# Seven products for eight in the second FFN product of two of three block pairs

## The chip, the cores and the metric

The kernel runs on one core of one Trainium2 chip. What counts is the device time of one execution in microseconds. TensorE multiplies matrices, VectorE and ScalarE do elementwise work, and SyncE (SP) issues the transfers between the chip's memory (HBM) and the core's own (SBUF). TensorE adds up its results in PSUM banks of 512 float32 columns.

## The reference

The inputs are q, k, v of shape (8, 8, 576, 64), a norm weight, and four matrices U (576, 32), V (32, 576), w_ch1 (512, 2048), w_ch2 (2048, 512).

```python
kv  = einsum('bhsd,bhde->bhse' of q with einsum('bhsd,bhse->bhde', k, v))   # linear attention
x   = kv / sqrt(mean(kv*kv, -1) + 1e-6) * g_norm                           # heads joined: (8, 576, 512)
u   = x + (x^T @ U @ V)^T                                                   # mixes the 576 tokens at rank 32
out = u + relu(u @ w_ch1) @ w_ch2                                           # the FFN
```

The matrices come as 64-bit floats and are cut to 32 bits in the kernel; the result is float32.

## The kernel before

The 8 x 576 tokens are one row of 4608, cut into nine blocks of 512. All work is transposed: features on the 128 partitions, tokens in the free dimension. A product keeps nearly float32 accuracy by splitting both factors into a high and a low part of the type float32r, and adding three matmuls: high x high, high x low, low x high. "Split" below means: ScalarE copies the high part (a cast), VectorE subtracts it from the value to give the low part.

Blocks 0 to 2 run the FFN in the ordinary way. Meanwhile the attention of the next sequences is done in small steps, a `pair_tasks` for each two heads; `at(h, ...)` puts such a step at step number h of the FFN, and `do(h)` emits what stands there. Blocks 3 to 8 run as three pairs, (3, 4), (5, 6) and (7, 8).

In a pair the first product, u @ w_ch1, goes by the Strassen-Winograd scheme. The hidden 2048 features are 16 chunks of 128; chunk n and chunk n + 8 form a *chunk pair*, and the four blocks A11 to A22 of a 2 x 2 matrix are the two chunks by the two halves of the 512 input features. With the other factor's four blocks (two halves of the features by two token blocks) seven products give what eight would: the weight forms `A11 A12 S2 S1 S3 S4 A22` with the forms of u `B11 B21 T2 T1 T3 B22 T4`. Each is 2 x 3 = 6 matmuls for a chunk pair. The weight's sums S1 to S4 are made once, in blocks 1 and 2, by `forms_of_w`, split, and stored in HBM; the forms of u are made by `forms_of_u` before the pair starts and stay in SBUF.

The chunk pairs are taken two at a time (`NPP = 2`), in `NG = 4` groups. For a group, the loop over the seven forms does `product` for both chunk pairs; `after` copies or adds the results into `sums` and, for each of the four hidden blocks 11, 12, 21, 22, runs `relu_to`: high part by ScalarE, low part by VectorE, into `hs`. Two PSUM banks serve a chunk pair, x and y: A11, S2, S3 and A22 add to x; A12 starts y; S1 starts y anew, so it may start only when A12's result has been read; S4 adds to it.

Then the second product of the group, `y_units`: eight units (two token blocks by four output chunks of 128), each 4 x 3 = 12 matmuls with the plain w_ch2, added by VectorE into the pair's running sum r (which starts as u). In the last group the sums go to `st` and out to HBM.

Weight forms come through `ring`, eight slots of 256 KB: `load_form(k + 7)` asks for the piece seven ahead after piece k is used. The w_ch2 chunks of a group (four of 512 KB) come into `w2r` by `load_w2` at the end of the group before. All transfers are on SP's one queue, in order. On each engine the order is set at build time by a scheduler that works from its own costs and from the order of the code; at run time each engine keeps that order. In the tables here `mm` is line 85, `add` line 542, the parts of `relu_to` lines 464 and 465, `load_form` line 520, `load_w2` line 527, and the forms of the weight lines 233 to 244.

Of the kernel before, what the change touches and what calls it, by code (L numbers as in the profile page):

```python
# [10 lines left out]
F32 = mybir.dt.float32  # L11
F32R = mybir.dt.float32r
# [23 lines left out]
STEPS = dict(kv=0, out=2, turn=3, t=5, mix=8)  # L36
STEPS0 = dict(kv=1, out=2, turn=2, t=6, mix=11)
PAIRS = {1: (0, 3, 6, 9), 2: (33, 39, 45, 51), 3: (64, 67, 70, 73), 4: (75, 78, 81, 84),
         5: (98, 103, 109, 114), 6: (120, 125, 131, 136), 7: (162, 169, 176, 183)}
# [4 lines left out]
RING = 8  # L44
FORMS = ["A11", "A12", "S2", "S1", "S3", "S4", "A22"]
# [11 lines left out]
def build(ctx: ExitStack, tc: tile.TileContext, kv_in, kvt0_in, kvt_in, q_in, uv_in, g_in, w_in, out):  # L57
# [7 lines left out]
    st = ctx.enter_context(tc.tile_pool(name="st", bufs=3))  # L65
    dec = ctx.enter_context(tc.tile_pool(name="dec", bufs=2))
# [109 lines left out]
    w1d, w2d = {}, {}  # L176
# [41 lines left out]
    def forms_of_w(n):  # L218

        c = DM // 2  # L220
        a = dec.tile([P, 2 * DM], F32, name="dec")
        for k, f in enumerate((n, n + HALF)):
            if f == 0:
                d1, d2 = [to_dram(f"{which}d0", whole[which, 0]) for which in ("w1", "w2")]
                w = whole["w1", 0]
            else:
                d = to_dram(f"wd{f}", whole[f])
                d1, d2 = d[:, 0:2], d[:, 2:4]
                w = whole[f][:, 0:2]
            w2d[f] = d2  # L230
            for i in range(2):
                w1d[n, f"A{k + 1}{i + 1}"] = d1[:, i]
            nc.vector.tensor_tensor(out=halves(a[:, k * DM:(k + 1) * DM]), in0=w[:, :, 0].bitcast(F32), in1=w[:, :, 1].bitcast(F32), op=ALU.add)
        a11, a12, a21, a22 = (a[:, k * c:(k + 1) * c] for k in range(4))
        ts = {}

        def form(name, in0, in1, op):
            t = ts[name] = st.tile([P, 2, c], F32R, name="st")
            nc.vector.tensor_tensor(out=t[:, 1].bitcast(F32), in0=in0, in1=in1, op=op)
            nc.scalar.copy(out=t[:, 0], in_=t[:, 1].bitcast(F32))  # L240

        def low(name):
            t = ts.pop(name)
            nc.vector.tensor_tensor(out=t[:, 1], in0=t[:, 1].bitcast(F32), in1=t[:, 0].bitcast(F32), op=ALU.subtract)
            w1d[n, name] = to_dram(f"w{name}_{n}", t)

        form("S1", a21, a22, ALU.add)
        form("S2", ts["S1"][:, 1].bitcast(F32), a11, ALU.subtract)
        low("S1")
        form("S4", a12, ts["S2"][:, 1].bitcast(F32), ALU.subtract)  # L250
        low("S2")
        form("S3", a11, a21, ALU.subtract)
        low("S4")
        low("S3")

    ut = {}
    rs = {}

# [603 lines left out]
```

## Time and profile before

| | us |
|---|---|
| median of 3 runs (903.16 to 905.18) | 903.65 |
| profiled execution | 902.88 |
| its span, first to last instruction | 901.1 |
| TensorE busy | 876.8 (97%) |
| VectorE busy | 561.3 (62%) |
| ScalarE busy | 313.5 (35%) |
| share of the transfer engines, main queue | 55.8% |
| mean granted TensorE clock | 0.994 |

Matmuls are pipelined: a row's mean duration (389 ns) is longer than the distance from one to the next, so the price of a matmul is read from a stretch without gaps, its length by its count. The first pair starts near 367 us, the second near 559, the last near 735; the last matmul ends near 898. "PE" is TensorE, "PEld" its weight loads, "DVE" VectorE, "ACT" ScalarE, "SPq" the transfer queue of SP. L85 stands for the line of the kernel, and `y<-hs,w2r` for a matmul from hs and w2r into the bank y.

### The profile page before, as it was taken

The numbers are of one execution on the slowest core, as the hardware profiler recorded it, in microseconds if no ns is written. First come the engines' busy times: TensorE is split into PE (matmuls) and PEld (weight loads), VectorE is DVE, ScalarE is ACT, GpSimd is POOL, SyncE is SP. The second block draws the span as 40 slices with busy tenths as digits, with TensorE's granted clock in tenths as the row PEclk, the third lists the DMA queues.
The fourth block names the chain that finished last, engine by engine and source line by source line (L and its number), as shares of the span: only waits on it lengthen the run. The fifth ranks groups of instructions, "written<-read, shape, count | busy, mean of one in ns | idle before, by whom it ended". The sixth has DMA issues, their size and how long they took to land.

```text
span 901.1 us, 12196 instructions
## 1 busy us (share of the span) xinstructions
PE 876.8 (97%) x4370; PEld 734.7 (82%) x4370; DVE 561.3 (62%) x1089; ACT 313.5 (35%) x629; POOL 22.3 (2%) x43
## 2 busy tenths in 40 slices
PE   8799999989999999999999999999999999999998
PEld 7678878778888878888888888888888888888887
DVE  6999996667866676475647666557452754243342
ACT  5545542333333434433424153324141422213030
POOL 2000002000020000200000000000000000000000
PEclk9899999999999999999999999999999999999999
DMA  9962123998575544766648384748282654527142
GB/s 339 407 263 80 46 79 106 367 381 337 199 232 151 145 118 113 228 188 209 212 147 290 86 267 143 249 124 265 56 254 73 208 194 133 183 75 219 38 164 94
DMA packets 81852, 168.11 MB, mean 187 GB/s; under 512 B 9216, under 2 KB 27392, under 8 KB 79872
## 3 DMA queue, kind: packets, MB, share of 16 engines
q1 hardware_dynamic: 81792, 167.33, 55.8%
q8 instruction: 35, 0.57, 0.3%
q14 instruction: 25, 0.20, 0.1%
HBM read 124.44 MB, written 42.86 MB: 186 GB/s over the span
## 4 chain that ended last, share of the span: by engine, by line
PE 85%; DVE 10%; DMA 2%; issue 1%; SPq 1%; ACT 1%; DVEq 0%; ACTq 0%
PE y L85 64%; PE h L85 11%; PE pp L85 9%; DVE dec L105 1%; DMA ut<-xt 1%; DVE dec L107 1%; DMA kvq<-kv_in 1%; DVE hl L465 1%; DVE ws L113 1%; DVE dec L102 1%; DVE x L338 1%; DVE dec L103 1%; DVE xt L366 0%; DVE ss L326 0%; DVE ut L446 0%
## 5 line engine op out<-in xcount | busy, mean ns | idle before, releaser
L85 PE MATMUL y<-hs,w2r 128*128 128x512 f32 (+1 forms) x1164 | 268.5, 389 | 0.0
L85 PEld LDWEIGHTS y<-hs,w2r 128*128 128x128 f32 x1164 | 215.4, 188 | 43.5
L85 PE MATMUL h<-uth,ws 128*128 128x512 f32 x360 | 122.1, 400 | 3.3 <-DVE hl L465 2.9
L85 PE MATMUL y<-hh,ws 128*128 128x512 f32 x360 | 118.9, 394 | 0.0
L85 PEld LDWEIGHTS h<-uth,ws 128*128 128x128 f32 x360 | 68.3, 190 | 20.2 <-DVE hl L465 6.4
L85 PEld LDWEIGHTS y<-hh,ws 128*128 128x128 f32 x360 | 67.2, 188 | 13.7
L85 PE MATMUL h<-utl,ws 128*128 128x512 f32 x180 | 70.8, 394 | 0.0
L85 PE MATMUL y<-hl,ws 128*128 128x512 f32 x180 | 70.1, 390 | 0.0
L85 PE MATMUL y<-uT,ringw 128*128 128x512 f32 x282 | 67.0, 389 | 0.0
L85 PE MATMUL y<-uT,ring 128*128 128x512 f32 x276 | 65.9, 390 | 0.0
L85 PEld LDWEIGHTS y<-uT,ringw 128*128 128x128 f32 x282 | 52.6, 188 | 10.7
L542 DVE TENSOR_TENSOR uth<-y,uth 128x512 f32<-128x512 f32 x36 | 24.9, 691 | 58.2 <-PE y L85 58.1
L85 PEld LDWEIGHTS y<-uT,ring 128*128 128x128 f32 x276 | 51.5, 188 | 10.6
L542 DVE TENSOR_TENSOR utl<-y,utl 128x512 f32<-128x512 f32 x36 | 24.9, 691 | 48.4 <-PE y L85 48.3
L85 PE MATMUL y<-uB,ring 128*128 128x512 f32 x216 | 52.1, 391 | 0.0
L549 ACT COPY sums<-y 128x512 f32<-128x512 f32 x23 | 13.4, 586 | 108.7 <-PE y L85 108.4
L85 PE MATMUL y<-uB,ringw 128*128 128x512 f32 x210 | 50.4, 391 | 0.0
L542 DVE TENSOR_TENSOR sums<-y,sums 128x512 f32<-128x512 f32 x48 | 32.7, 688 | 23.6 <-PE y L85 18.7
L85 PEld LDWEIGHTS y<-uB,ring 128*128 128x128 f32 x216 | 40.2, 188 | 8.2
L464 ACT ACTIVATE hh<-h 128x512 fp32r<-128x512 f32 x47 | 28.0, 596 | 52.2 <-PE h L85 52.0
L85 PEld LDWEIGHTS y<-uB,ringw 128*128 128x128 f32 x210 | 39.2, 188 | 8.1
L542 DVE TENSOR_TENSOR dec<-y,dec 128x512 f32<-128x512 f32 x23 | 15.9, 692 | 44.8 <-PE y L85 37.9
(200 smaller groups left out, 1208.2 us busy)
## 6 DMA issues: line engine op xcount, KB each, us to landing
w2r<-wd SPq DMA_DIRECT2D x45, 512.0 KB, 6.1
raw<-w_in SPq DMA_DIRECT2D x30, 512.0 KB, 10.2
wd<-ws SPq DMA_DIRECT2D x15, 1024.0 KB, 8.0
kv_sb<-kv_in SPq DMA_DIRECT2D x29, 512.0 KB, 3.9
ring<-wS SPq DMA_DIRECT2D x48, 256.0 KB, 4.5
ringw<-wS SPq DMA_DIRECT2D x48, 256.0 KB, 4.4
ring<-wd SPq DMA_DIRECT2D x36, 256.0 KB, 3.8
out<-st SPq DMA_DIRECT2D x35, 256.0 KB, 2.0
```

The costliest lines, as they stand in the source:

```text
L85: ins = nc.tensor.matmul(*args, **kw)
L102: nc.vector.tensor_scalar(out=tmp, in0=tmp, scalar1=ABS_LO, scalar2=ABS_HI, op0=ALU.max, op1=ALU.min)
L103: nc.vector.tensor_scalar(out=bits, in0=bits, scalar1=3, scalar2=0x3fffffff, op0=ALU.logical_shift_left, op1=ALU.bitwise_and)
L105: nc.vector.scalar_tensor_tensor(out=bits, in0=high, scalar=0xC0000000, in1=bits, op0=ALU.bitwise_and, op1=ALU.bitwise_or)
L107: nc.vector.scalar_tensor_tensor(out=bits, in0=low, scalar=29, in1=bits, op0=ALU.logical_shift_right, op1=ALU.bitwise_or)
L113: lo_eng.tensor_tensor(out=lo, in0=src, in1=hi.bitcast(F32), op=ALU.subtract)
L338: nc.vector.tensor_tensor(out=xv[:, 0:4], in0=s["big"].rearrange("p (i h e) -> p i h e", h=2, e=D), in1=rv[:, 0:4].unsqueeze(3).broadcast_ ...
L464: nc.scalar.activation(out=hh, in_=h, func=AF.Relu)
L465: nc.vector.scalar_tensor_tensor(out=hl, in0=h, scalar=0.0, in1=hh.bitcast(F32), op0=ALU.max, op1=ALU.subtract)
L542: nc.vector.tensor_tensor(out=out, in0=in0, in1=in1, op=ALU.add)
L549: nc.scalar.copy(out=s[0], in_=x)
```

## The change

The second product of pairs (5, 6) and (7, 8) goes by the same seven-product scheme. There the 2 x 2 matrix of the weight has two halves of the 512 outputs by two chunks, and the other factor is the hidden activation with its blocks 11, 12, 21, 22. The pair (3, 4) keeps its form.

- Groups are four chunk pairs (`NR = 4`), two groups a pair. A group does two rounds of the first product, `round_of_ffn1`, two chunk pairs each, and then the seven forms of the second, `product2`: for each form two output chunks i, and for each i the four chunk pairs by three matmuls, 24 matmuls a form, all adding up in one bank for each i.
- `after_both` takes the place of `after`: it leaves the relu'd blocks h11, h12, h22, h21 whole in float32. `form_of_h` then makes the forms of h: "sums1" and "sums2" the differences, three and one VectorE instructions of 1024 columns for two chunk pairs, and for each of the seven forms and each two chunk pairs a split into `entry` tiles (four of them, so a form has two and the next form the other two; two of the four lie in the pools `dec` and `hhl`). The first two forms are split within and just after the rounds, form n + 2 after the product of form n.
- `after2` adds each result to the running sum: 14 adds a group in place of 16 for the same chunk pairs; the last is not cut in two halves any more.
- The weight's sums for the second product are made in the first pair: `sums_of_w("w2", ...)` for each of the eight chunk pairs, from the `w2r` tiles loaded there, in two steps placed between the first pair's units. Step one adds high and low parts back to whole values and makes four differences; step two splits them (`dec`, `wf`) and stores them with two transfers of 512 KB. The sums for the first product are made by the same function now, at every third step in place of every second.
- All weight forms of the last two pairs, for both products, come through the ring in 256 KB pieces: `load_upto(k + 8)`. `w2r` is loaded for the first pair alone.
- Steps of the attention for blocks 5 to 7 move by one, and for blocks 5 to 7 the steps t and mix come two later (`STEPS2`).

```diff
+BOTH = (5, 7)
+NR = 4
...
+        def one():
+            t["plain"] = a = dec.tile([P, 2 * DM], F32, name="dec")
+            for k, w in enumerate(get()):
+                nc.vector.tensor_tensor(out=halves(a[:, k * DM:(k + 1) * DM]), in0=w[:, :, 0].bitcast(F32), in1=w[:, :, 1].bitcast(F32), op=ALU.add)
+            a11, a12, a21, a22 = (a[:, k * c:(k + 1) * c] for k in ((0, 1, 2, 3) if which == "w1" else (0, 2, 1, 3)))
+            for o, in0, in1, op in ((a22, a21, a22, ALU.add), (a21, a11, a21, ALU.subtract), (a11, a22, a11, ALU.subtract),
+                                    (a12, a12, a11, ALU.subtract)):
+                nc.vector.tensor_tensor(out=o, in0=in0, in1=in1, op=op)
+
+        def two():
+            hi = dec.tile([P, 2 * DM], F32R, name="dec")
+            lo = wf.tile([P, 2 * DM], F32R, name="wf")
+            split(hi, lo, t["plain"], nc.vector)
+            d = dram.tile([P, 4, 2, c], F32, name=f"{which}s{n}")
+            for s, part in enumerate((hi, lo)):
+                nc.sync.dma_start(out=d[:, :, s], in_=part.bitcast(F32).rearrange("p (a c) -> p a c", a=4))
...
+    def load_upto(end):
+
+        for k in range(len(loaded), min(end, len(pieces))):
+            t = loaded[k] = sb["ring"][k % RING]
+            nc.sync.dma_start(out=t.bitcast(F32), in_=wd[pieces[k]])
...
+    def form_of_h(name, q):
+
+        two = slice(2 * q, 2 * q + 2)
...
+        if name == "sums1":
+            nc.vector.tensor_tensor(out=h11, in0=h12, in1=h11, op=ALU.subtract)
+            nc.vector.scalar_tensor_tensor(out=t2, in0=h22, scalar=0.0, in1=h11, op0=ALU.max, op1=ALU.subtract)
+            nc.vector.scalar_tensor_tensor(out=h12, in0=h22, scalar=0.0, in1=h12, op0=ALU.max, op1=ALU.subtract)
+        elif name == "sums2":
+            nc.vector.tensor_tensor(out=h21, in0=h21, in1=t2, op=ALU.subtract)
+        else:
+            hi, lo = entries[name, q] = sb["entry"][(2 * WITH.index(name) + q) % len(sb["entry"])]
+            src = {"B11": h11, "B21": h21, "T2": t2, "T1": h11, "T3": h12, "B22": h22, "T4": h21}[name]
...
+                nc.scalar.copy(out=hi, in_=src)
+                nc.vector.tensor_tensor(out=lo, in0=src, in1=hi.bitcast(F32), op=ALU.subtract)
+
+    def product2(k, n, i, bank, first):
+
+        for r in range(NR):
+            w = loaded[k + r].rearrange("p s (i f) -> p s i f", i=2)
+            hi, lo = (t[:, r % 2] for t in entries[WITH[n], r // 2])
+            for m, (s, t) in enumerate(((0, hi), (0, lo), (1, hi))):
+                mm(bank, lhsT=w[:, s, i], rhs=t, start=(first and r == 0 and m == 0), stop=(r == NR - 1 and m == 2),
+                   skip_group_check=not first)
...
+            round_of_ffn1(j, g, 0, after_both)
+            for name in ("B11", "B21"):
+                form_of_h(name, 0)
+            round_of_ffn1(j, g, 1, after_both)
+            form_of_h("B11", 1)
+            form_of_h("B21", 1)
+            form_of_h("sums1", 1)
+            form_of_h("sums2", 1)
...
+                    product2(k, n, i, banks[i, which], FORMS[n] in ("A11", "A12", "S1"))
+                    after2(n, i, banks[i, 0], banks.get((i, 1)), j, g == HALF // NR - 1)
+                k += NR
+                load_upto(k + RING)
+                if n + 2 < len(FORMS):
+                    for q in range(2):
+                        form_of_h(WITH[n + 2], q)
```

Three places show how the change moves instructions. The first is TensorE at the end of the last pair. Before, the last form of the first product (uT with a ring slot) is followed by units that take hs and w2r; the last rows of the kernel are these:

```order
L85 MATMUL y<-hs_3574,w2r_3577 128x512 x3
L85 MATMUL y<-hs_3572,w2r_3576 128x256 x3
L85 MATMUL y<-hs_3572,w2r_3577 128x256 x3
L85 MATMUL y<-hs_3574,w2r_3576 128x256 x3
L85 MATMUL y<-hs_3574,w2r_3577 128x256 x3
```

Now, from the last form of the last round on:

```order
L90 MATMUL y<-uT_3007,ringw_2535 128x512 x12
L90 MATMUL y<-entry_5177,ring 128x512 x6
L90 MATMUL y<-entry_5178,ring 128x512 x6
L90 MATMUL y<-entry_5177,ring 128x512 x6
L90 MATMUL y<-entry_5178,ring 128x512 x6
L90 MATMUL y<-dec,ringw_2534 128x512 x6
L90 MATMUL y<-hhl,ringw_2535 128x512 x6
```

Each form takes 24 matmuls from two of the four entry tiles, and the ring's slots now feed both products.

The second place is VectorE in the first pair, where one group's units end and the next group's first forms are read. L542 into uth is the unit's add, L542 into sums the add that reads A12's bank (line 556 after the change); ss, ta, r and x are steps of the attention. Before:

```order
L542 TENSOR_TENSOR uth<-y,uth 128x512
L326 TENSOR_REDUCE ss<-x 128x10
L542 TENSOR_TENSOR sums<-y,sums 128x512
L328 RECIPROCAL r_4481<-ta 128x10
L329 TENSOR_TENSOR ta<-r_4481 128x10
L330 SCALAR_TENSOR_TENSOR ta<-ss,ta 128x10
L542 TENSOR_TENSOR sums<-y,sums 128x512
```

Now, from right behind the last unit's add:

```order
L248 TENSOR_TENSOR dec<-w2r_3427 128x512
L397 TENSOR_TENSOR t_4357<-pp,t_4357 32x128
L336 TENSOR_REDUCE ss<-x 128x10
L248 TENSOR_TENSOR dec<-w2r_3427 128x512
L338 RECIPROCAL r_4371<-ta 128x10
L252 TENSOR_TENSOR dec<-dec 128x256
L339 TENSOR_TENSOR ta<-r_4371 128x10
L252 TENSOR_TENSOR dec<-dec 128x256
L340 SCALAR_TENSOR_TENSOR ta<-ss,ta 128x10
L252 TENSOR_TENSOR dec<-dec 128x256
L341 SCALAR_TENSOR_TENSOR r_4371<-ta,r_4371 128x10
L556 TENSOR_TENSOR sums<-y,sums 128x512
```

Two adds that read the new group's w2r (L248) and three of the differences (L252) have come between the last unit's add and the add that reads A12's bank.

The third is VectorE behind the second product of the last pair, from the first results on:

```order
L556 TENSOR_TENSOR uth<-y,uth 128x512
L639 TENSOR_TENSOR h_5175<-h_5175,t_5176 128x1024
L648 TENSOR_TENSOR entry_5177<-t_5176,entry_5177 128x1024
L556 TENSOR_TENSOR uth<-y,uth 128x512
L648 TENSOR_TENSOR entry_5178<-t_5176,entry_5178 128x1024
L556 TENSOR_TENSOR st<-y,uth 128x512
L648 TENSOR_TENSOR dec<-h_5172,dec 128x1024
```

Low parts of 1024 columns (L648) alternate with the adds of results, where before only the units' adds stood.

More of the change, by code (lines that the diff above doesn't have):

```diff
@@ L228, in forms_of_w @@
                 d1, d2 = d[:, 0:2], d[:, 2:4]
-                w = whole[f][:, 0:2]
+                ws.append(whole[f][:, 0:2])
             w2d[f] = d2
             for i in range(2):
[L232 to L240, printed above, removed]
@@ L458, in relu @@
     def relu(h):
[L459 to L461 removed]
+        t = hp.tile([P, 2, BLK], F32R, name="hhl")
+        relu_to(t[:, 0], t[:, 1], h)
+        return t[:, 0], t[:, 1]
     def relu_to(hh, hl, h):
@@ new lines, in product2, with after2 @@
+    def product2(k, n, i, bank, first):
[5 more added lines that the diff above has]
+                   skip_group_check=not first)
+    def after2(n, i, x, y, j, last):
+        name = FORMS[n]
+        src = y if name in ("A12", "S1", "S4") else x
+        part = int(name in ("S2", "S1", "S3", "S4"))
+        c = i + 2 * int(name in ("S1", "S3", "A22"))
+        own = r_of(j + part)[:, c]
+        if last and name in ("A12", "S3", "S4", "A22"):
+            o = st.tile([P, DM], F32, name="st")
+            add(o, src, own)
+            nc.sync.dma_start(out=out[j + part, c], in_=o)
+        else:
+            add(own, src, own)
@@ L774, in build, with round_of_ffn1 @@
     h = 32 * NSTD
-    for j in range(NSTD, NBLK, 2):
-        for g in range(NG):
+    def round_of_ffn1(j, g, q, done):
+        nonlocal k, h
+        banks = {}
+        for n in range(len(FORMS)):
+            do(h)
+            h += 1
+            for a in range(2):
+                early = k == 0
+                if n == 0:
+                    banks[a, 0] = ps_p.tile([P, BLK], F32, name="pp") if early else ps_y.tile([P, BLK], F32, name="y")
+                elif n == 1:
+                    banks[a, 1] = ps_y.tile([P, BLK], F32, name="y")
+                which = int(FORMS[n] in ("A12", "S1", "S4"))
+                product(k, n, banks[a, which], FORMS[n] in ("A11", "A12", "S1"))
+                k += 1
+                if early:
+                    ffn2(y_prev, [hprev])
+                    finish(y_prev, NSTD - 1)
+                    sb_tiles("rest")
+                    sb_tiles("ring2")
+                    load_w2(0)
+                done(n, 2 * q + a, banks[a, 0], banks.get((a, 1)))
+                load_upto(k + RING)
+            if q == 1 and n in (1, 3):
+                form_of_h(f"sums{n // 2 + 1}", 0)
```

157 lines of the change are left out of this document (93 added, 64 removed).

## The prediction

> **What bounds the kernel now.** I read the page's first part, then the windows over the last three pairs of blocks, then the chain of waits and TensorE's own waits.
>
> ```profile
> PE 876.8 (97%) x4370; PEld 734.7 (82%) x4370; DVE 561.3 (62%) x1089; ACT 313.5 (35%) x629; POOL 22.3 (2%) x43
> PEclk9899999999999999999999999999999999999999
> ```
>
> ```profile
> core 0: us, PE busy (x) PEld busy (x) DVE busy (x) ACT busy (x) POOL busy (x), PEclk, DMA share, GB/s
> 150.00:200.00 50.00, 47.43 (x249) 39.85 (x247) 32.54 (x75) 15.98 (x39) 4.68 (x4) 1.00 0.93 354
> ...
> 405.00:570.00 165.00, 164.38 (x830) 138.32 (x829) 102.03 (x205) 60.39 (x122) 0.00 (x0) 1.00 0.63 200
> 570.00:736.00 166.00, 166.00 (x799) 138.87 (x798) 94.33 (x172) 51.38 (x98) 0.00 (x0) 1.00 0.51 161
> 736.00:901.00 165.00, 162.09 (x727) 134.52 (x725) 59.42 (x89) 34.02 (x56) 0.00 (x0) 1.00 0.42 141
> ```
>
> The last three rows are most of the first pair, the second (from near 559 us) and the third. TensorE is busy through all of them, at full clock, while VectorE falls from 62% to 57% to 36%. The chain of waits ends in one unbroken stretch of TensorE, and its waits from 405 us to the last matmul come to 0.6 us:
>
> ```profile
> 666.74 231.36 PE y L85 x1032
> ```
>
> ```profile
> PE pp L85 <- DVE xh L354: 0.6, 1, 0.6
> ```
>
> So in the pairs the time is the number of matmuls times their spacing. Of the 1032, 24 have half the columns, so 231.36 / 1020 = 0.2268 us for each full one. What the change removes there is worth its full spacing, as long as the new forms, sums and loads keep up.
>
> **The change, part by part.**
>
> *1. Fewer matmuls.* One pair's second product takes 4 groups x 8 units x 12 = 384 full matmuls now, and 2 groups x 7 forms x 2 x 12 = 336 after. Two pairs: 96 fewer, 96 x 0.2268 = **-21.8 us**. The first product keeps its 336. Lower bound: if the spacing were not the matmul's own but that of what feeds it, a removed one would be worth the weight load's 188 ns, 96 x 0.188 = 18.0 us.
>
> ```profile
> L85 PEld LDWEIGHTS y<-hs,w2r 128*128 128x128 f32 x1164 | 215.4, 188 | 43.5
> L465 DVE SCALAR_TENSOR_TENSOR hs<-sums,hs 128x512 fp32r<-128x512 f32 x48 | 32.7, 687 | 2.5 <-ACT hs L464 1.3
> ```
>
> The Trainium skill (TensorE: Matmul & The Clock Gate, section Back-to-back issue gap) has a sustained spacing of about 131 ns for 512 columns in a stream of weight loads and matmuls; by it the saving would be 96 x 0.131 = 12.6 us, an estimate from that page. This trace does not agree (0.2268 us over 1020 matmuls), and the measurement decides.
>
> *2. Work for VectorE and ScalarE in the last two pairs.* Prices:
>
> ```profile
> L113 DVE TENSOR_TENSOR ws<-dec,ws 128x1024 fp32r<-128x1024 f32 x15 | 18.2, 1219 | 0.7 <-ACT ws L112 0.6
> L542 DVE TENSOR_TENSOR uth<-y,uth 128x512 f32<-128x512 f32 x36 | 24.9, 691 | 58.2 <-PE y L85 58.1
> L244 DVE TENSOR_TENSOR st<-st 128x256 fp32r<-128x256 f32 x32 | 13.1, 422 | 3.8 <-ACT st L240 2.9
> ```
>
> ```profile
> L112 ACT CAST ws<-dec 128x1024 fp32r<-128x1024 f32 x15 | 15.8, 1051 | 24.5 <-DVE dec L107 17.5 <-DVE ta L330 4.8 <-DVE r L331 2.1
> L464 ACT ACTIVATE hs<-sums 128x512 fp32r<-128x512 f32 x48 | 30.2, 631 | 25.9 <-DVE sums L542 25.8
> ```
>
> Per pair VectorE loses 32 low parts of 512 (32 x 0.687 = 22.0) and 4 adds (2.8), and gains 28 low parts of 1024 (28 x 1.219 = 34.1) and 16 sums of 1024 (19.5): +28.8 us. The last pair goes from 59 to 88 us busy of about 154 (57%), the second from 94 to 123 of about 155 (79%). ScalarE gains 28 casts of 1.051 and loses 8 relus of 0.631, +24 us: 75 of 155 at most. Neither becomes the bound on average; what counts is whether a form is late at its place.
>
> In the second product each form is 24 matmuls, 24 x 0.2268 = 5.44 us. Behind it VectorE must do two low parts and two adds, 2 x 1.219 + 2 x 0.691 = 3.8 us, and ScalarE two casts, 2.1 us; a form's first tile is free at three quarters of the product two before, so cast, low part, cast, low part have 1.4 + 5.4 us for 1.05 + 2 x 1.22 plus waits. In the last pair that leaves over 2 us. In the second pair the attention of block 7 runs on VectorE too. Adding rows in program order I find the narrowest places in its second group: S1 of the second round restarts a bank whose reading add ends 0.4 us earlier, and T3's second half is ready 1.5 us before its use. Bounds: 0 (all fit) to 6 us (two late forms in each of the two groups, each by one 1.219 us and wait); I take **+1**, nearer the row sums, which fit.
>
> *3. The second-product forms, made in the first pair.* For each of 8 chunk pairs VectorE gets two adds of 512, four of 256 and one low part of 1024: 2 x 0.691 + 4 x 0.422 + 1.219 = 4.3 us, in all 34 us, and ScalarE one cast. VectorE's 102 us of 165 becomes about 131 (80%). SP gets 16 stores of 512 KB. The cost is in the order: the two adds that read w2r's new contents stand ahead of the adds of A12, and VectorE works in order. So a late weight load now holds VectorE, then A12's bank, then S1, which starts that bank anew. Before, the loads had until the end of the seven forms. The group from 467 us:
>
> ```profile
> 467.19 2.06 SPq L527 DMA_DIRECT2D w2r<-wd  x4
> 468.74 2.88 PE L85 MATMUL y<-uB,ring 128*128 128x512 f32 x12
> 474.16 0.69 DVE L542 TENSOR_TENSOR sums<-y,sums 128x512 f32<-128x512 f32 x1
> 475.54 0.69 DVE L542 TENSOR_TENSOR sums<-y,sums 128x512 f32<-128x512 f32 x1 [0.16 <-PE y L85]
> 475.61 5.61 PE L85 MATMUL y<-uT,ringw 128*128 128x512 f32 x24
> ```
>
> ```profile
> L527 SPq DMA_DIRECT2D w2r<-wd x12: 319/351/444, 416.0 to 518.9; - x12
> DMA to landing us min/median/max: 3.9/6.5/9.0
> ```
>
> The third of the four loads is issued at about 468.2 and lands at 474.7 (median) or 477.2 (longest). Then come the second w2r add, three differences and the small statistics (0.69 + 1.27 + 0.5 = 2.5), A12's first add (0.69, ends 477.9 or 480.4) and, after 0.42 + 0.96, the second (479.9 or 482.4). S1 starts at about 475.61 + 2.72 = 478.35, its second half at 479.7. So TensorE waits 0.2 us at the median and 2.7 us at the longest. Three such places: 0 to 8 us. I take 1 each, **+3**, between the median and the longest because the stores load the queue further. The first group's loads are issued long before its start, and VectorE's wait for an output transfer there gives cover.
>
> *4. Loads in the last two pairs.* A pair loads 112 pieces of 256 KB, 29.4 MB, in 672 x 0.2268 = 152 us: 193 GB/s, beside 354 that the 150 to 200 us row shows at a share of 0.93. A piece of the second product frees its slot in the second half of its form, and the piece that takes the slot is wanted 33 matmuls or 7.5 us later. Landing times now:
>
> ```profile
> L520 SPq DMA_DIRECT2D ring<-wd x36: 319/320/422, 379.2 to 865.3; - x36
> ...
> DMA to landing us min/median/max: 2.7/4.4/8.2
> ```
>
> The median leaves 3 us, which hides it, with SP's issue at about 0.4 us each. A longest one costs 0.7. Bounds 0 to 2; I take 0. Without that cover every form would wait (a rival below).
>
> *5. The first-product forms* in blocks 1 and 2 are spread over every third step, with one low part of 1.219 for four of 0.422 and one cast for four. VectorE saves 0.5 us a chunk pair. TensorE's idle time from 100 to 400 us, most of those blocks, is 300 less 291.99:
>
> ```profile
> 100.00:200.00 100.00, 96.45 (x481) 79.07 (x479) 75.53 (x147) 36.20 (x73) 5.13 (x4) 1.00 0.56 202
> 200.00:300.00 100.00, 98.30 (x513) 83.45 (x514) 71.15 (x170) 36.33 (x89) 5.07 (x4) 0.98 0.67 230
> 300.00:400.00 100.00, 97.24 (x518) 81.72 (x517) 65.83 (x143) 40.36 (x87) 5.10 (x4) 1.00 0.55 164
> ```
>
> Of these 8 us a shifted order may win or add a quarter. Bounds -2 to +2; I take 0.
>
> *6. The end.* The last add is now 512 wide and the last store 256 KB:
>
> ```profile
> 898.13 0.42 DVE L542 TENSOR_TENSOR st<-y,uth 128x256 f32<-128x256 f32 x1 [1.01 <-PE y L85]
> ```
>
> ```profile
> out<-st SPq DMA_DIRECT2D x35, 256.0 KB, 2.0
> ...
> out<-st SPq DMA_DIRECT2D x2, 128.0 KB, 1.7
> ```
>
> 0.69 - 0.42 + 2.0 - 1.7 = **+0.6**.
>
> Sum: -21.8 + 1 + 3 + 0 + 0 + 0.6 = -17.2. The profiled execution took 902.88 us, 1.8 more than its span; 902.9 - 17.2 = 885.7. The median of the runs shown stands 0.8 above it, so I predict 886.5.
>
> **The rivals.**
>
> A. *All of it hides*: the loads land as at the median, no form is late. Only parts 1 and 6 are left, -21.2, perhaps with up to 2 us from part 5: 880.5 to 882.5. For it: TensorE does not wait on VectorE now in the pairs. Against: VectorE goes to 80%, in order.
>
> B. *VectorE becomes the bound locally* in the first and second pair: parts 2 and 3 at their upper ends, +6 + 8 + 0.6 - 21.8 = -7.2, 896.5. For it: the margins of 0.2 and 0.4 us. Against: one late form does not delay the next, since the mean load is below 80%.
>
> C. *Slower: the ring of eight is too short for the second product.* There a form frees all four slots only in its last half. It decides once a load lands later than 7.5 us after its slot is free; the 28 forms of the two pairs' four groups each pay what is beyond that. To undo 17.2 us takes 0.6 us a form, so landing at 8.1 us as the usual case: about today's longest. At 9.0 us it is 28 x 1.5 = 42 us, and 903.7 - 17.2 + 42 = 928.5. For it: eight pieces are always asked for, and SP waits in order behind transposes. Against: 193 GB/s is well below what the queue has moved.
>
> D. *A removed matmul is worth less than its spacing*, the weight load's 188 ns: -18.0 + 4.6, so 890.3. The page's 131 ns would be such a rule. Against: 1020 matmuls at one spacing, with no wait between.
>
> **How the numbers follow.** My forecast (882.5 to 891) 0.58; A 0.21; B (891 to 900) 0.14; C 0.05; D 0.02. The likeliest is 886.5. The range 880.5 to 897 holds A, the forecast and most of B. About 0.2% (1.8 us) can be told from no change here; C holds the slower cases and a rest of B and C the same: faster 0.94, same 0.02, slower 0.04.
>
> **What would show it.** The last stretch of TensorE in the chain should have no gap and keep 0.2268 us; matmuls of the second product 96 fewer. In the first pair TensorE should wait for VectorE's sums at S1, 0 to 2.7 us at a group, with VectorE waiting for w2r loads just before. In the second pair waits on entry, dec or hhl are at most 1.5 us. The last pair should last 152 to 153 us. I am wrong if ring loads release TensorE in the last pair, if its clock row drops, or if waits in blocks 1 and 2 change by more than 2 us.

## The result and the profile after

The changed kernel takes 897.08 us in the median of 8 runs (893.49 to 898.29), the kernel before 905.8 us in the runs beside them: a ratio of 0.9892 with a 95% interval of 0.9866 to 0.9919. By this ratio it is faster by about 9.8 us, 1.1% (the two medians lie 8.7 us apart). The profiled execution takes 894.29 us with a span of 892.5, against 902.88 and 901.1 before: 8.6 us less, where the prediction had 17.2. The median stands 0.1 us above the upper end of the predicted range (the runs of the kernel before beside it are 2.2 us above those that the forecast started from; by the ratio, 903.65 x 0.9892 = 893.9 us, which is inside). The direction was right, and half of the gain is missing.

The first part of the page after:

```profile
PE 859.4 (96%) x4262; PEld 715.6 (80%) x4262; DVE 643.3 (72%) x1136; ACT 361.1 (40%) x653; POOL 23.9 (3%) x43
```

TensorE's busy time fell by 17.4 us, but the span by 8.6: its idle time grew from 24.3 to 33.1 us. To see where, I cut both traces at the same matmuls. The first five columns run over the FFN's 512-column matmuls of blocks 0 to 2 in their order (384 a block): the start of the first one, then the time from the first to the 97th, to the 289th, to the 577th (the last quarter of block 0 and the first half of block 1), and to the first matmul of the first pair. Then the three pairs, each from its first matmul with uB to that of the next, and what lies behind the last matmul. The kernels e1 to e11 are those of the experiments below.

| us | start | 1-97 | 97-289 | 289-577 | to pair | pair (3,4) | pair (5,6) | pair (7,8) | end | span |
|---|---|---|---|---|---|---|---|---|---|---|
| before | 38.97 | 29.20 | 55.22 | 82.98 | 160.76 | 191.81 | 175.65 | 163.51 | 3.01 | 901.11 |
| after | 40.07 | 29.15 | 55.21 | 85.73 | 161.07 | 197.85 | 166.37 | 152.93 | 4.14 | 892.52 |
| e1 no forms made | 39.39 | 29.87 | 56.27 | 85.83 | 161.02 | 191.16 | 166.37 | 152.48 | 4.14 | 886.53 |
| e2 adds only | 39.16 | 29.08 | 55.21 | 85.87 | 160.94 | 192.31 | 166.37 | 152.48 | 4.12 | 885.55 |
| e3 pinned | 42.16 | 30.81 | 55.30 | 85.86 | 162.43 | 194.40 | 166.38 | 152.48 | 4.13 | 893.94 |
| e4 w1 as before | 43.41 | 30.88 | 55.97 | 82.74 | 162.39 | 198.95 | 166.38 | 152.48 | 3.66 | 896.86 |
| e5 forms behind units | 39.27 | 30.43 | 55.68 | 82.97 | 161.07 | 191.16 | 166.38 | 153.76 | 3.02 | 883.72 |
| e6 step later | 40.17 | 30.16 | 55.95 | 82.75 | 162.28 | 191.16 | 164.65 | 154.02 | 3.02 | 884.16 |
| e7 forms in blocks | 40.22 | 30.10 | 56.04 | 82.93 | 176.44 | 191.15 | 166.38 | 153.40 | 3.02 | 899.69 |
| e8 both out | 41.70 | 30.83 | 55.23 | 84.58 | 160.86 | 191.16 | 166.38 | 152.48 | 3.67 | 886.88 |
| e9 finish on VectorE | 40.62 | 30.73 | 55.37 | 94.94 | 160.86 | 197.80 | 166.37 | 152.48 | 3.64 | 902.81 |
| e10 e6 without the cut | 39.07 | 30.55 | 55.54 | 83.05 | 161.15 | 191.15 | 164.65 | 152.48 | 3.67 | 881.31 |
| e11 e10, finish on VectorE | 41.61 | 30.80 | 55.28 | 81.14 | 163.33 | 191.15 | 164.65 | 152.48 | 3.65 | 884.09 |

Read the columns downwards. The pairs repeat to some hundredths of a microsecond from kernel to kernel where their work and order are the same, while the start moves by up to 4.4 us and the first quarter by up to 1.8 us between executions, whatever the kernel. So a difference in a pair's column is one execution's evidence already, and a difference of whole times of 2 us is not.

Between before and after, then: start +1.1; the last quarter of block 0 to the middle of block 1 +2.75; first pair **+6.04**; second -9.28; last -10.58; end +1.13; the rest +0.3. Sum -8.6.

The windows over the same three pairs after (columns as in the prediction):

```profile
371.00:569.00 198.00, 193.68 (x974) 160.16 (x973) 152.53 (x303) 74.60 (x150) 5.62 (x4) 1.00 0.71 231
569.00:735.50 166.50, 165.05 (x795) 138.06 (x794) 120.02 (x182) 79.95 (x129) 0.00 (x0) 1.00 0.68 212
735.50:888.40 152.90, 152.76 (x673) 125.85 (x671) 88.46 (x99) 57.79 (x77) 0.00 (x0) 1.00 0.62 203
```

The last pair is what was forecast: full clock, TensorE without a pause but for some 0.4 us at its start, VectorE at 58%. The chain of waits shows the same as one stretch, 0.2272 us for each of 660 matmuls:

```profile
738.45 149.95 PE y L90 x660
```

In the first pair VectorE is busy 77%, near the 80% of the forecast, and TensorE waits for it. TensorE's waits there, and the two groups of VectorE's own waits that matter:

```profile
PE y L90 <- DVE hs L475: 3.4, 6, 1.6
PE y L90 <- DVE sums L556: 0.6, 1, 0.6
```

```profile
DVE uth L556 <- PE y L90: 13.7, 10, 2.0
DVE dec L248 <- DMA w2r<-wd: 9.9, 5, 3.0
```

VectorE does wait for the w2r loads (9.9 us in five waits), which the prediction had named. But the bank that S1 restarts, where this was to show, cost TensorE one wait of 0.6 us. The waits are in another place: `hs L475`, the low part of a hidden block that a unit multiplies. In time order, the end of the seven forms and the start of the units of the second group, VectorE first and TensorE behind it:

```profile
445.38 0.42 DVE L252 TENSOR_TENSOR dec<-dec 128x256 f32<-128x256 f32 x1
...
447.07 0.69 DVE L475 SCALAR_TENSOR_TENSOR hs<-sums,hs 128x512 fp32r<-128x512 f32 x1
447.67 1.23 DVE L118 TENSOR_TENSOR wf<-dec 128x1024 fp32r<-128x1024 f32 x1
448.80 0.69 DVE L348 TENSOR_TENSOR x<-pp,r 128x512 f32<-128x512 f32 x1
449.40 0.27 DVE L350 TENSOR_TENSOR x<-pp,r 64x128 f32<-64x128 f32 x1
449.60 0.67 DVE L475 SCALAR_TENSOR_TENSOR hs<-y,hs 128x512 fp32r<-128x512 f32 x1
450.20 0.67 DVE L475 SCALAR_TENSOR_TENSOR hs<-sums,hs 128x512 fp32r<-128x512 f32 x1
```

```profile
446.92 2.43 PE L90 MATMUL y<-hs,w2r 128*128 128x512 f32 x10
450.93 0.74 PE L90 MATMUL y<-hs,w2r 128*128 128x512 f32 x2 [1.58 <-DVE hs L475]
```

The units start at 446.92 and need the low part of the last hs at their eleventh matmul. VectorE has the making of the w2 forms (L252, then wf of L118) and the attention's x between the low parts, so that low part ends at 450.87, and TensorE stands for 1.58 us. The code puts the making between the units; the scheduler has put it ahead, among the forms. In the kernel before, the units of this group start at 441.38, and their eleventh matmul comes at about 443.65; the last low part ends at 443.44, and they run on:

```profile
442.77 0.67 DVE L465 SCALAR_TENSOR_TENSOR hs<-y,hs 128x512 fp32r<-128x512 f32 x1
```

```profile
441.38 2.89 PE L85 MATMUL y<-hs,w2r 128*128 128x512 f32 x12
```

The waits listed for the first pair come to 4.3 us, with one of 0.3 for st; the pair lost more. A wait is counted from the modelled end of the matmul before it; from start to start the places with waits in these rows cost about 0.27 us more each. All that the matmuls of the pair start later than their usual spacing comes to 8.7 us here and 2.3 us in e1, where the pair is 6.7 us shorter, and that is nearly all of it.

The other loss, in block 0's last chunks, is on VectorE too. Its rows from 151.94 us, and TensorE's:

```profile
151.94 1.88 DVE L488 TENSOR_TENSOR st<-y,uth 128x512 f32<-128x512 f32 x3
153.74 1.41 DVE L118 TENSOR_TENSOR wf<-dec 128x1024 fp32r<-128x1024 f32 x1
155.18 1.27 DVE L298 TENSOR_TENSOR tails<-kvt_sb,tails 64x128 fp32r<-64x128 f32 x1
156.46 1.29 DVE L299 TENSOR_TENSOR tails<-kvt_sb,tails 128x128 fp32r<-128x128 f32 x1
...
158.27 1.29 DVE L248 TENSOR_TENSOR dec<-ws 128x512 f32<-128x512 f32 x2
...
160.66 0.68 DVE L488 TENSOR_TENSOR st<-y,uth 128x512 f32<-128x512 f32 x1
```

```profile
156.83 2.20 PE L90 MATMUL y<-hhl,w2s 128*128 128x512 f32 x9
161.40 0.97 PE L90 MATMUL y<-hhl,w2s 128*128 128x512 f32 x3 [2.36 <-DVE st L488]
```

Three of block 0's four finishing adds (L488) run at once; the fourth stands behind a low part of the w1 forms, two small instructions of the attention's tails and the next chunk pair's adds, 8.7 us after the first. Its bank is the one that block 1's second product waits for. In the kernel before, the fourth comes 5.4 us after the first (148.71 us), behind the tails alone:

```profile
154.07 0.69 DVE L478 TENSOR_TENSOR st<-y,uth 128x512 f32<-128x512 f32 x1
```

The wait of 2.36 us is the largest part of what the stretch from the 289th to the 577th matmul loses, and not the whole: in this stretch TensorE stands still for 6.6 us, nearly all in eight places, against 4.7 us in three before. The new order adds this one and some of about 0.6 us, and the two waits for the attention's ut, 1.6 and 2.6 us before, are 1.0 us each.

### The profile page after: what moved, and what is told of

The parts are those of the page before. It is cut to its first block, busy times and chain, and to the rows that moved or that the text cites. A ratio compares the mean times of both kernels' runs of the same rounds, so it can differ in the third digit from the quotient of the medians.

```text
span 892.5 us, 12229 instructions
## 1 busy us (share of the span) xinstructions
PE 859.4 (96%) x4262; PEld 715.6 (80%) x4262; DVE 643.3 (72%) x1136; ACT 361.1 (40%) x653; POOL 23.9 (3%) x43
## 4 chain that ended last, share of the span: by engine, by line
PE 71%; DVE 19%; DMA 5%; issue 2%; ACT 1%; SPq 1%; DVEq 0%; ACTq 0%
PE y L90 53%; PE h L90 10%; PE pp L90 8%; DMA w2r<-wd 2%; DVE dec L110 1%; DVE dec L252 1%; DVE hhl L475 1%; DVE dec L248 1%; DVE hs L475 1%; DVE dec L112 1%; DMA ringw<-w1s 1%; DVE x L348 1%; DMA w1raw<-w_in 1%; DVE ws L118 1%; DVE ss L336 1%
## 5 line engine op out<-in xcount | busy, mean ns | idle before, releaser
L90 PE MATMUL y<-hhl,ws 128*128 128x512 f32 x540 | 133.0, 392 | 0.0
L90 PEld LDWEIGHTS y<-hhl,ws 128*128 128x128 f32 x540 | 100.0, 188 | 20.3
L90 PE MATMUL y<-hs,w2r 128*128 128x512 f32 x384 | 93.1, 394 | 3.4 <-DVE hs L475 3.4
L90 PE MATMUL y<-entry,ring 128*128 128x512 f32 x384 | 90.3, 390 | 0.0
L90 PEld LDWEIGHTS y<-hs,w2r 128*128 128x128 f32 x384 | 70.5, 188 | 19.9 <-DVE hs L475 6.2
L90 PEld LDWEIGHTS y<-entry,ring 128*128 128x128 f32 x384 | 71.8, 188 | 14.7
L556 DVE TENSOR_TENSOR h<-y,h 128x512 f32<-128x512 f32 x48 | 32.9, 688 | 45.0 <-PE y L90 43.0
L475 DVE SCALAR_TENSOR_TENSOR hhl<-h,hhl 128x512 fp32r<-128x512 f32 x47 | 32.3, 687 | 33.0 <-ACT hhl L474 32.7
L648 DVE TENSOR_TENSOR entry<-h,entry 128x1024 fp32r<-128x1024 f32 x24 | 29.3, 1221 | 22.3 <-ACT entry L647 22.2
L90 PE MATMUL pp<-kvb,q_sb 128*128 128x128 f32 x280 | 37.8, 281 | 2.0 <-DVE ut L456 2.0
L125 ACT CAST xh<-x 128x640 fp32r<-128x640 f32 x30 | 21.8, 728 | 43.1 <-DVE x L350 41.8
L90 PEld LDWEIGHTS h<-utl,ws 128*128 128x128 f32 x180 | 34.2, 190 | 6.3
```

Of the source, the lines that this page charges most:

```text
L90: ins = nc.tensor.matmul(*args, **kw)
L125: nc.scalar.copy(out=out, in_=in_)
L475: nc.vector.scalar_tensor_tensor(out=hl, in0=h, scalar=0.0, in1=hh.bitcast(F32), op0=ALU.max, op1=ALU.subtract)
L556: nc.vector.tensor_tensor(out=out, in0=in0, in1=in1, op=ALU.add)
L648: nc.vector.tensor_tensor(out=lo, in0=src, in1=hi.bitcast(F32), op=ALU.subtract)
```

## The experiments

**e1 and e2: is it the forms made in the first pair, and is it the wait or the work?** e1 drops the making, e2 keeps only the two adds that read w2r:

```diff
-                    if m % 4 < 2:
-                        prep[m // 4][m % 4]()
```

```diff
     for k, w in enumerate(get()):
         nc.vector.tensor_tensor(out=halves(a[:, k * DM:(k + 1) * DM]), in0=w[:, :, 0].bitcast(F32), in1=w[:, :, 1].bitcast(F32), op=ALU.add)
+    if which == "w2":
+        return
...
-                    if m % 4 < 2:
+                    if m % 4 < 1:
                         prep[m // 4][m % 4]()
```

> The changed kernel without the making of the second-product weight sums in the first pair: no adds, differences, splits and stores there; in the last two pairs the sums of the first product's weights are loaded in their place (same size, same count), so that the values are wrong and the work of the last two pairs is the same. Theory 1 (the making of these forms costs the first pair its 6.0 us): the first pair falls from 197.85 us to 191.8 +- 0.5, TensorE's waits for hs in it disappear, and the whole falls by about 6 us. Rival (the first pair is longer for another reason, the shifted attention steps or the ring asked one piece further ahead): the first pair stays above 195 us. Both: last pair stays 152.9, blocks 0 to 2 as in the changed kernel (their order is the same), so the first pair starts at 371.2 if these 4.1 us belong to the order, and near 368 if they were that one execution's.

> As the first, but the two adds that read w2r stay in each chunk pair (11 us of work in all, and the wait for the weight load at their head); the four differences, the split and the stores are left out, and the sums of the first product's weights stand in, so the values are wrong. Theory 1a (the length of the work, 34 us put ahead of the low parts in VectorE's order, delays the first pair): about a third of the 6 us or less is left, first pair 192 to 194 us. Theory 1b (the wait for the w2r load at the head of VectorE, 11.7 us in the changed kernel's first pair, delays it): most of the 6 us stays, first pair 196 to 198 us.

Measured: e1 889.66 us (ratio 0.9817, 0.9782 to 0.9853), first pair 191.16; e2 891.68 us (0.9829, 0.9788 to 0.9871), first pair 192.31. So the making costs the first pair 6.7 us, of which the adds with their wait for the load are 1.15. The wait itself is all there in e2: of VectorE's waits in its first pair,

```profile
DVE dec L248 <- DMA w2r<-wd: 9.2, 7, 2.6
```

9.2 us of waiting for w2r cost TensorE little more than one microsecond. Theory 1b, and with it the mechanism that I had predicted, falls; 1a stands: it is the 34 us of work in that order (34 is the sum of the rows; VectorE's busy time in the pair is 123.7 us in e1 and 152.5 with the making). In e1 the first pair starts at 372.38, and the column 289-577 shows 85.83, as in the changed kernel: that part of the later start belongs to the order and is no accident of one execution.

**e3: the same work, in another order.** The first pair's adds, low parts and the making of the forms are held in the code's order:

```diff
-        nc.vector.tensor_tensor(out=out, in0=in0, in1=in1, op=ALU.add)
+        keep_dve(nc.vector.tensor_tensor(out=out, in0=in0, in1=in1, op=ALU.add))
...
+    def keep_dve(ins):
+        if dve[0]:
+            tc.keep_in_program_order(ins)
...
+        dve[0] = j not in BOTH
```

> The changed kernel with VectorE's adds and low parts of the first pair and its making of the second-product forms held in the order of the code, so that the forms' instructions stand among the units' adds and no longer among the seven forms' adds and low parts. All the work and all the loads stay. Theory 1a and 1b both: the units' start no longer waits, the first pair falls to 192 to 193 us and the whole by 5 us. Rival (VectorE, or the stores on SP's queue, are too much for the first pair wherever they stand): 196 us or more, with the waits moved to the units' banks.

Measured: 895.39 us (0.9867, 0.9836 to 0.9898), first pair 194.40: 3.45 of 6.7 us came back, between the two expectations. TensorE's waits in its first pair:

```profile
PE y L95 <- DVE hhl L562: 2.1, 2, 1.3
PE y L95 <- DVE hs L481: 0.6, 1, 0.6
```

The low parts are nearly in time; the new waits are for adds of the seven forms. Those too were held in the code's order, and stand behind the attention's instructions there. Whether the rest was the work or the holding, this run left open.

**e4: the first-product forms as before.** Each chunk pair again by four casts and four low parts of 256 columns, at every second step:

```diff
-        for m, what in enumerate(sums_of_w("w1", n, lambda n=n: copy_of_w(n))):
-            at(35 + 3 * n + m, what)
+        at(35 + 2 * n, lambda n=n: forms_of_w(n))
```

> The changed kernel with the first-product weight sums made as before the change (four casts, four low parts of 256 columns, four stores for a chunk pair, every second step). Theory 2 (the new order of these forms costs blocks 0 to 2 about 3 us, by the finishing adds of block 0 that wait behind them on VectorE): the first pair starts at 367.5 to 368.5 instead of 371.2, the wait of 2.4 us for st near 161 us is gone, the rest is unchanged, the whole falls by 3 us. Rival (those 4.1 us are that execution's, by its slower start and a half-clock spell): the start of the first pair is no earlier than in the runs that keep the new order.

Measured: 894.03 us (0.9862, 0.9819 to 0.9905). The stretch 289-577 is 82.74 us against 85.73 to 85.87 in the four traces with the new order, and the wait for st is gone: the fourth finishing add comes 5.4 us after the first again. Theory 2 holds, for about 3 us of this stretch. The whole times alone would not show it, since the intervals of this run and of the changed kernel overlap. The two waits for ut are back (4.1 us). The edit puts back the size of the instructions and their steps together, so which of the two made the order is not shown. The expected start of the first pair (367.5 to 368.5) missed: 375.39, since this execution began its FFN at 43.41 and was 1.7 us slower up to the 97th matmul. The first pair became 1.1 us longer than in the changed kernel, with one wait of 2.2 us for the same low parts.

**e5: both repairs, and the cut at the end.** As e4; in the first pair only the units' adds and the making keep their order, the seven forms are free; and the last result is cut in halves:

```diff
+                    dve[0] = True
                     y_unit(j, *unit)
                     if m % 4 < 2:
                         prep[m // 4][m % 4]()
+                    dve[0] = False
...
+                    for cols in ([slice(0, BLK // 2), slice(BLK // 2, BLK)] if end else [slice(0, BLK)]):
+                        product2(k, n, i, banks[i, which], FORMS[n] in ("A11", "A12", "S1"), cols)
+                        after2(n, i, banks[i, 0], banks.get((i, 1)), j, g == HALF // NR - 1, cols)
```

> Three edits at once on the changed kernel: in the first pair only the units' adds and the making of the second-product forms keep the code's order on VectorE (the seven forms' adds and low parts are free again); the first-product forms are made as before the change; the last result of the last pair is cut in two halves again. Theory 1a (VectorE's order in the first pair) says: first pair 191.5 to 193 us, the rest of the 3.2 us that the full pinning left over came from the pinning. Rival (the 34 us of work cost the first pair 3 us wherever they stand, of VectorE's or the stores' load): 194 to 195 us. Theory 2: from the first matmul of block 0's last quarter to the end of block 1's first half 82.7 to 83 us (85.7 in the changed kernel). End: 0.5 to 1 us less after the last matmul. Sum of the three by the theories: 6 + 2.8 + 0.6 = 9.4 us below the changed kernel, about 887.

Measured: 885.98 us (0.9771, 0.9749 to 0.9793), first pair 191.16, which is e1's without any making. VectorE's busy time in that pair, from the windows, is what it was, and TensorE has one wait left:

```profile
370.40:561.60 191.20, 190.85 (x974) 160.86 (x973) 151.70 (x304) 77.23 (x150) 5.17 (x4) 1.00 0.72 233
```

```profile
PE y L95 <- DVE hs L509: 0.4, 1, 0.4
```

151.7 us of VectorE work in 191.2 us here, 152.5 in 198 in the changed kernel. So all 6.7 us were the order, none the amount, and e3's rest was the holding (the first-product forms, which e5 changes too, did not shorten the pair in e4). The same place in time, with the last low part first and the making behind it:

```profile
445.99 0.68 DVE L509 SCALAR_TENSOR_TENSOR hs<-y,hs 128x512 fp32r<-128x512 f32 x1
447.51 1.28 DVE L253 TENSOR_TENSOR dec<-w2r 128x512 f32<-128x512 f32 x2
```

The end behaved differently than expected: 3.02 us behind the last matmul instead of 4.14, but the last pair is 153.76 instead of 152.48 in e1 to e4. Of this 0.5 us is a wait: the second half waits for the first half's add in the same bank:

```profile
879.01 1.69 PE L95 MATMUL y<-entry,ring 128*128 128x256 f32 x12 [0.52 <-DVE st L590]
```

In the kernel before, the two halves had a bank each.

**e6: the wait of the second pair.** The t step of the last sequence's second heads comes two steps later:

```diff
+            ... dict(STEPS2, t=9, mix=12) if (b, p) == (7, 1) else STEPS2
```

> As the one before, and the t step of the second heads of the last sequence's attention comes two steps later. Theory 3 (the single wait of 1.5 us in the second pair, near 626 us, is that step's matmul waiting for xh, which VectorE makes late behind the splits of the first forms): the wait is gone or below 0.3 us, the second pair falls from 166.4 to 164.9 us. Rival (VectorE as a whole is behind at that place): the wait moves to a bank or an entry tile and the pair keeps its 166.4.

The one wait of that pair in e5, as in the changed kernel:

```profile
PE pp L95 <- DVE xh L398: 1.5, 1, 1.5
```

In e6 it is gone, nothing takes its place, and the pair falls from 166.38 to 164.65. The whole takes 884.22 us (0.9755, 0.9739 to 0.9771). Theory 3 holds: not VectorE's load, but one instruction put two steps too early.

**e7: the forms made elsewhere.** In blocks 1 and 2, from the weights that lie there:

```diff
-                    if m % 4 < 2:
-                        prep[m // 4][m % 4]()
...
+        for m, what in enumerate(sums_of_w("w2", n, ...whole...)):
+            at(60 + 3 * n + m, what)
```

> The second-product forms made in blocks 1 and 2 from the weights that lie there, behind the first-product forms, and not in the first pair; first-product forms and the end as before the change. No load is waited for. By the measured cost of the first-product forms' order in blocks 0 to 2 (2.8 us for a shift alone) theory 1a expects that 34 us more on VectorE, at 71 to 75% there, cost 2 to 6 us in blocks 1 and 2, and that the first pair falls to 191 us. Rival (the place is free there, since the blocks wait mostly on ScalarE and PSUM): first pair at 191 us and blocks 1 and 2 no longer than before the change, the whole near 884.

Measured: 902.96 us (0.9953, 0.9926 to 0.9981). The first pair is at 191.15 as both sides said; blocks 1 and 2 are 15.4 us longer than in e5, far above either. Its windows and waits there:

```profile
260.00:300.00 40.00, 36.69 (x195) 31.06 (x194) 38.32 (x83) 15.76 (x34) 5.84 (x4) 0.96 0.86 269
300.00:340.00 40.00, 30.35 (x165) 25.29 (x164) 33.80 (x77) 16.02 (x35) 0.00 (x0) 0.91 0.66 205
```

```profile
PE pp L90 <- DVE ut L484: 4.9, 4, 1.7
PE pp L90 <- DVE x L376: 3.4, 3, 1.4
PE y L90 <- DVE st L516: 2.6, 1, 2.6
```

From 260 to 300 us VectorE is busy 96%; what it falls behind with is the attention (ut, x) and a finishing add (st), for which TensorE stops. TensorE's waits from the middle of block 1 to the pair are 10.5 us more than in e5. Most of the rest goes with the granted clock, 0.96 and 0.91 in the two windows: that is 5 us of lost clock in 80. The mean of 71 to 75% over blocks 1 and 2 had told me too little.

**e8: both costs out at once.**

> No making of the second-product forms (the first product's sums stand in for them, so the values are wrong) and the first-product forms as before the change. If the two costs are independent, both are gone: first pair 191 to 191.8 us, 82.7 to 83 us from the last quarter of block 0 to the first half of block 1, last two pairs 166.4 and 152.9; this is the changed kernel with all its new preparation hidden, 6.7 + 2.8 us below it at the same start.

One execution: 888.74 us, pairs 191.16, 166.38 and 152.48 as expected. The stretch 289-577 is 84.58, not 83: its two waits of 2.1 and 2.2 us there are each followed by seven matmuls at twice the usual spacing, of which more below. The kernels before, e4 to e7 and e10, with the same order of these forms, have one such series there and take 82.74 to 83.05 us.

**e9 and e11: the second finishing add on VectorE instead of GpSimd; e10: e6 without the cut.**

```diff
-            nc.gpsimd.tensor_tensor(out=o, in0=o, in1=ul[:, c, :].bitcast(F32), op=ALU.add)
+            nc.vector.tensor_tensor(out=o, in0=o, in1=ul[:, c, :].bitcast(F32), op=ALU.add)
```

> The changed kernel with the second add of a block's finish moved from GpSimd to VectorE (12 instructions; 1.4 to 1.6 us each on GpSimd, 0.69 us on VectorE by the 512-column adds there). Theory 4 (the two small VectorE instructions that make the tails' low parts near 155 us took 1.27 and 1.29 us instead of 0.29 because GpSimd was adding at the same time, and this is part of the wait of 2.4 us): no such instruction is above 0.4 us in the trace, the fourth finishing add comes earlier by about 2 us less 2 x 0.69, and the stretch from the last quarter of block 0 to the middle of block 1 falls from 85.7 to 84.5 to 85.3 us. Rival (they were slow for another reason, a transfer or their place): an instruction of them stays near 1.3 us.

> The kernel of e6 with the last result whole, as in the changed kernel. The cut kernel's trace shows the second half waiting 0.5 us for the first half's add in the same bank, 154.0 us for the last pair and 3.0 behind it; whole it was 152.5 and 4.1 in the first experiment. So the two should stand within 0.5 us of each other: 883.8 to 885, and the cut is worth nothing in this form. Rival (the cut gains its 1.1 us behind the last matmul): 885.5.

> The kernel of e10 with the second add of a block's finish on VectorE. If theory 4 holds also where the first-product forms are made as before the change, blocks 0 to 2 win what the slow tails cost there, up to 1 us; VectorE gets 12 x 0.69 us more, spread over three blocks. Between 883 and 885.5, no difference that can be told from e10 if the finishing adds have cover there.

e9: 905.66 us (0.9979, 0.9961 to 0.9998). The mechanism is as theory 4 said. Durations of the two tails instructions (min, median, max), in the changed kernel and in e9:

```profile
L298 DVE TENSOR_TENSOR tails<-kvt_sb,tails x24: 287/289/1270, 120.6 to 629.5; 64x128 fp32r<-64x128 f32 x24
```

```profile
L298 DVE TENSOR_TENSOR tails<-kvt_sb,tails x24: 289/290/291, 122.9 to 640.7; 64x128 fp32r<-64x128 f32 x24
```

The consequence was wrong: the stretch 289-577 grew to 94.94 us. With other costs the scheduler made another order. Now the fourth finishing add comes 10.7 us after the first, 1.0 us of it waiting for an output transfer. Near 196 us the attention's ut stands behind a low part of the w1 forms, which itself waits 6.1 us for the store of an earlier one:

```profile
PE pp L90 <- DVE ut L456: 8.3, 3, 7.0
PE y L90 <- DVE st L488: 4.4, 1, 4.4
```

The granted clock from 160 to 215 us is 0.88, so the long waits cost more than their own length.

e10 takes 885.45 us (0.9751, 0.9726 to 0.9777), e11 884.85 (0.9746, 0.9728 to 0.9763): neither can be told from e6. In e10 the last pair and the end together are 156.15 us, in e6 157.04, so the cut in one bank gains nothing. In e11 the stretch 289-577 wins 1.9 us against e10 (81.14), and 2.2 are lost behind it: there e11 waits 0.7 us more, and has a spell of half clock (below) that e10 does not have. The best of these kernels, e6, e10 and e11, take 22 to 23 us less than the one before, more than twice what the change alone gives.

## Why the prediction was half right

*Part 1, the matmuls* (-21.8): right. Without other losses the last pair takes 163.51 - 152.48 = 11.0 us less, the second in e6 175.65 - 164.65 = 11.0. That is 0.2295 us for each of 96. The lower bound of 188 ns (rival D) was no bound: at the end of the kernel before, the 24 half-width matmuls, with a weight load each, start 0.120 us apart. The Trainium skill's 131 ns (TensorE: Matmul & The Clock Gate, section Back-to-back issue gap) does not agree with this stream either.

*Part 2, late forms in the last pairs* (+1, bounds 0 to 6): near. +1.7 us in the second pair (166.37 against e6's 164.65), at another place: no form is late, but the attention's xh behind the forms' low parts, a wait of 1.5 us (e6). The last pair loses 0.45 us (152.93 against 152.48), nearly all at its start. One of the second pair's last adds into st waits for an output transfer, and the first weight load of the last pair's second form waits for that add:

```profile
737.70 0.69 DVE L556 TENSOR_TENSOR st<-y,uth 128x512 f32<-128x512 f32 x1 [1.72 <-DMA out<-st]
```

```profile
738.44 1.70 PEld L90 LDWEIGHTS y<-uB,ringw 128*128 128x128 f32 x8 [0.54 <-DVE st L556]
```

In e5 and e6 the same row waits 0.5 and 0.7 us. No run was made to take this wait away.

*Part 3, the forms made in the first pair* (+3): the term that was mis-sized, and its mechanism was wrong. It measured +6.0, 6.7 against the pair without any making. I took the order of the listing at one place, the two adds ahead of A12's, followed the load's landing from there to S1, and did not follow the rest of VectorE's rows to the next consumer, the units. The load's wait, on which the sum rested, costs 1.2 us together with the two adds (e2); the one wait for sums is 0.6 us, where the sum had 1 us at each of three places.

*Part 4, the ring* (0): right, and rival C falls: no ring load releases TensorE in the last two pairs, and the longest landing of a ring load in the changed kernel is 7.9 us beside a median of 3.6 to 3.8.

*Part 5, the first-product forms* (0, bounds -2 to +2): wrong, +2.75 us, outside the bounds (e4). I compared amounts of work (0.5 us less a chunk pair) where the order counted. In the new order more of the forms' work stands ahead of a finishing add (8.7 us from the first to the fourth, 5.4 before and in e4).

*Part 6, the end* (+0.6): right where the last stores land in the 2.0 us that the sum took for them (e8: 3.67 - 3.01 = 0.66). In the profiled execution of the changed kernel the stores of the last 16 us took 2.8 in the median, and the end +1.1. A cut in the same bank is no remedy (e6, e10).

The rest of the difference, 1.4 us, is the later start of that execution and its waits up to the first pair, which move by more than that from run to run. What was missing, in the order of the time: start and ends of blocks 0 to 2 1.4, part 5 2.75, part 3 3.0, part 2 0.6, 0.3 in the last pair (at its start, under part 2), part 6 0.5. Sum 8.6 us, the whole. Rival B came nearest in time (VectorE bound locally, 896.5), but e5 shows it isn't VectorE's load: with all of it, in a better order, the kernel is where rival A had it (903.65 x 0.9755 = 881.5 for e6). That the result lies at the range's upper end, or inside it by the ratio, is luck: the range was wide enough there to hold most of B, and B's reason is not what happened.

## What to carry to other kernels

A cost that "hides" on an engine which works in order is a question of what stands behind it in the queue, not of the mean load: at 77 to 79% busy it cost 6.7 us in one order and nothing in another. Follow every row that is put ahead to the next consumer of that engine, beyond the first one that waits, and hold the added work behind the rows that feed the bound engine; hold only the added work, since holding its neighbours too cost half the gain. Work that is moved to another stage is to be priced by that stage's fullest part and not by its mean: in e7 the mean there had been 71 to 75%, but the work filled 40 us of it to 96%, and it cost 15.4 us where it saved 6.7.

## What the runs showed of the hardware

*Waits of 2 us may cost some 1.6 us more.* In the changed kernel and in e1 TensorE waits the same 2.00 us at the same place. Its rows behind that wait, in the changed kernel and in e1:

```profile
67.28 0.50 PE L90 MATMUL h<-uth,ws 128*128 128x512 f32 x1 [2.00 <-DVE hhl L475]
...
68.54 0.62 PE L90 MATMUL h<-uth,ws 128*128 128x512 f32 x2
68.99 0.39 PE L90 MATMUL h<-utl,ws 128*128 128x512 f32 x1
```

```profile
66.73 0.50 PE L90 MATMUL h<-uth,ws 128*128 128x512 f32 x1 [2.00 <-DVE hhl L475]
...
68.84 0.63 PE L90 MATMUL h<-utl,ws 128*128 128x512 f32 x1
69.26 1.05 PE L90 MATMUL h<-uth,ws 128*128 128x512 f32 x2
```

In the one the matmuls go on at 0.227 us, in the other seven of them, from 68.41 us, start 0.427 us apart, and the window of 60 to 75 us shows a granted clock of 0.89 against 1.00 (0.51 from 68.0 to 71.4 us alone). In the ten traces of before, after and e1 to e8, ten of the eleven waits of 2.2 us and more behind 60 us are followed within 6 us of their end by two to seven such matmuls, and of the fourteen from 1.97 to 2.16 us nine are; the eleventh, of 2.20 us in e5, is followed by none. Single shorter waits are followed by none. Three waits of 0.55, 0.83 and 0.76 us within 15 us, which nine of the ten traces have between 306 and 329 us, were followed by them in e3, e4 and e6 and not in the six others; the longer series in e7 was followed by them too. Eight such matmuls last 8 x 0.427 = 3.4 us and cost 1.6. Much of the table's scatter goes with these spells. From the first matmul to the 289th (columns 1-97 and 97-289 together) it takes 84.3 to 84.4 us in before, after and e2, which have no spell behind the wait of 2 us near 67 us, and 86.1 to 86.9 in the ten others, which have one (its wait is near 71 us in e4). The column to the pair has 160.8 to 161.2 us in the eight traces without a spell there, and 162.3 to 163.3 in e3, e4, e6 and e11 with one. No run set out to change the spells by themselves. The Trainium skill (TensorE: Matmul & The Clock Gate, section What's actually happening) has a free-running window of about 3.4 us after which an idle engine falls to half the rate; the length of the spells and their chance beginning agree, but here waits of 2.0 us were enough, and sometimes were not.

*GpSimd slows VectorE's small instructions.* While GpSimd adds two tiles from SBUF (L489 in the changed kernel, 152.8 to 157.6 us), VectorE's 64x128 subtraction of two SBUF tiles takes 1.27 us instead of 0.29; without GpSimd's adds all 24 take 0.29 (e9). The kernel before has the same slow pair (0.93 and 1.29 us at 151.3 us, inside GpSimd's adds), so hardly any of this is what the change cost. The Trainium skill (SBUF — State Buffer, section Who interferes with whom) has VectorE's second SBUF input on a port shared with GpSimd; the traces agree.
